# An opening rebuilt: modulation weights from two queues, whole loads of the feature-DFT weights, narrow filler products, the first row pair in halves, weight differences on VectorE

## The chip, the core and the metric

The kernel runs on one core of a Trainium2 chip. It is one launch, and the time is the device time of that launch in microseconds. The kernel before took 716.78 us as the median of three runs (714.04 to 717.35). One further execution was recorded by the hardware profiler; it took 715.7 us from its first to its last instruction, and all views below are of it. Engines are called PE (TensorE's products), PEld (its weight loads), DVE (VectorE), ACT (ScalarE), POOL (GpSimd) and SP (SyncE, which here only issues loads).

## The reference

An adaLN-conditioned block over 2048 rows of 512 features: a Fourier mixing layer, then a SwiGLU layer (1792 hidden columns). The change touches the start of the first.

```
mod = (silu(c) @ w_mod).reshape(c.shape[0], 6, 1, -1)
sa, ca, ga, sb, cb, gb = (mod[:, 0], mod[:, 1], ..., mod[:, 5])
h = layernorm(x) * (1 + ca) + sa
a = einsum("bsd,ed->bse", h, dft_hid_re)        # feature DFT
b = einsum("bsd,ed->bse", h, dft_hid_im)
y = einsum("ts,bse->bte", dft_seq_re, a) - einsum("ts,bse->bte", dft_seq_im, b)   # sequence DFT
x = x + ga * y
h = layernorm(x) * (1 + cb) + sb
x = x + gb * (einsum(silu(h w1) * (h w3), w2))
```

## The kernel before

The work is one long function, `folded`, that writes out the program of all engines; each engine runs its own instructions in the order written, and waits for others by semaphores. It uses symmetries of the DFT: rows are taken in eight *row pairs* k (two sides of 128 rows each, the second the mirror of the first), and the features in four blocks dt of 128. Products in float32 are split into a high part and a low part (a rounded copy, and what is left), so that high x high, high x low and low x high make one product (`PASSES`).

**Loads.** SP issues, in this order: the condition `cc`, the rows x0 of pair 0, four blocks `wmr` of 512 KB of modulation weights (`load_wm`, L212), the feature-DFT weights `w` of block 0 (`load_hid`, L222), x1, w of blocks 1 to 3, x2 and x3. A block w[dt] is 128 partitions x 1024 numbers: 512 of the real matrix `wdr`, 512 of the imaginary `wdi`. In memory `w[i]` lies as 128 rows, each with two parts q of 512 numbers; `load_hid` takes every second row, part 0 to partitions 0 to 63 and part 1 to partitions 64 to 127, by two loads per matrix. For x4 to x7 one side comes from SP and the mirrored side by a gather that GpSimd issues (`load_mirror`, L165; L170).

**The opening's steps.** `mod_scale(v, h)` multiplies modulation weights by silu(c) (one ACT and three DVE instructions per v), `mod_sum(v)` sums over partitions on PE (L303) and writes the shift (v = 0) and the scale (v = 1) to `mod1` (L310). Filler products, `keep_warm` (L270), keep PE occupied meanwhile. For a row pair: statistics (`norm_stats`, L433), root, inverse, scaling, `turn_rows` (transposes on PE, L469), `modulate_rows` (L485 on ACT, L487 on DVE: `hm`), `mirror_sums` (`hs`: sum and difference of the two sides), `sum_highs` and `sum_lows` (`hh`, `hl`), `mirror_part` (`h1`). For a block of w: `w_highs` (ACT, `wu`), `w_lows` (DVE, L90 and L383), `w_minus` (ACT, `wn`), `differ_w` (POOL, L399 and L404, `wd`). `hid_product(k, dt)` (L533) then makes the low columns of the feature DFT: for k's first block a product with zeros clears the bank (L528), and for each half m (sum, difference) three passes follow. `hid_mirror` (L569) makes the high columns, `hid_difference` (L550) the correction with `wd`.

**The order.** The first pair's norm, turning and modulation sums are written out by hand. The rest of the opening is a table of tasks, each with a rank, needs and a cost per engine; `arrange` (L1284) takes again and again the task of lowest rank among those that can begin soonest by these costs and by due times for what is loaded (`at`, `clear`), and writes it. So costs and due times decide the order of the instructions on an engine, not when they run. After the opening, the sequence DFT (L723), the second norm and the SwiGLU layer (L100) follow.

Of the kernel before, what the change touches and what calls it, by code (L numbers as in the profile page):

```python
# [15 lines left out]
P = 128  # L16
# [26 lines left out]
def folded(nc, pools, c, cp, wmr, wmc, x, xt, ctr, cti, wdr, wdi, w1, w3, w2, out):  # L43
# [30 lines left out]
    def flat(t):  # L74
        return t.rearrange("p a b -> p (a b)")
# [10 lines left out]
    def copy(dst, src, scale=1.0):  # L86
        nc.scalar.activation(dst, src, AF.Copy, scale=scale)  # L87
# [122 lines left out]

    wm = {}

    def load_wm(v):
        for k in range(2):
            wm[v, k] = take(F32, "wmr")
            nc.sync.dma_start(wm[v, k], wmr[v, k])


    HD = ((0, 1), (1, 1), (0, 0), (1, 0))
# [2 lines left out]
    def load_hid(dt):  # L222
        i, par = HD[dt]
        raw_w[dt] = take(F32, "w")
        for m, w in enumerate((wdr, wdi)):
            for q in range(2):
                nc.sync.dma_start(raw_w[dt][q * 64 : (q + 1) * 64, m, :], w[i][par::2, q])

    nc.sync.dma_start(cc, cp)
    load_x(0)  # L230
    load_wm(1)
    load_wm(0)
    load_hid(0)
    load_x(1)
    for dt in range(1, ND):
# [30 lines left out]
    nc.vector.memset(onesf, 1.0)  # L266
    warm = bank(7)

    def keep_warm(count):

        for _ in range(count):
            nc.tensor.matmul(warm, onesf[:, :P], onesf, start=True, stop=True)

    sc = consts.tile([P, ND], F32, name="sc")
    nc.scalar.activation(sc, cc, AF.Silu)
# [24 lines left out]
    def mod_sum(v):  # L300

        for dt in range(ND):
            nc.tensor.matmul(  # L303
                mod_acc[:, v * ND + dt : v * ND + dt + 1],
                hid_cols(wm[v, 0][:, 0, :], dt),
                onesf[:, :1],
                start=True,
                stop=True,
            )
        nc.vector.tensor_scalar(  # L310
            mod1[:, v, :], mod_acc[:, v * ND : (v + 1) * ND], float(v), None, op0=OP.add
        )
        for h in range(2):
            give(wm.pop((v, h)))

# [76 lines left out]
    def differ_w(dt):  # L392
        r = quarters(raw_w[dt])
        if dt % 2 == 0:
            wd[dt // 2] = take(F32R, "wd")
        dd = wd[dt // 2][:, dt % 2, :].rearrange("p (a n) -> p a n", a=2)

        def pool(out, a, b, op):
            nc.gpsimd.tensor_tensor(out=out, in0=a, in1=b, op=op)  # L399

        if HD[dt][1]:
            pool(dd[:, 0, :], r[:, 0, 1, :], r[:, 0, 0, :], OP.add)
            pool(r[:, 1, 1, :], r[:, 1, 1, :], r[:, 1, 0, :], OP.add)
            nc.gpsimd.tensor_scalar(dd[:, 1, :], r[:, 1, 1, :], -1.0, None, op0=OP.mult)  # L404
        else:
            pool(dd[:, 0, :], r[:, 0, 1, :], r[:, 0, 0, :], OP.subtract)
            pool(dd[:, 1, :], r[:, 1, 0, :], r[:, 1, 1, :], OP.subtract)
        give(raw_w.pop(dt))

    def check_w(n):  # L410
# [83 lines left out]
            sides(hs[k])[:, :, m, :], sides(hm[k])[:, :, 0, :], sides(hm[k])[:, :, 1, :]  # L494
        )

    def sum_highs(k):
        hh[k] = take(F32R, "hh")
        copy(flat(hh[k]), flat(hs[k]))

    def sum_lows(k):
        hl[k] = take(F32R, "hl")
        minus(flat(hl[k]), flat(hs[k]), flat(hh[k]).bitcast(F32))
        give(hs.pop(k))

    def mirror_part(k):

# [13 lines left out]
    def halves(b):  # L521
        return b.rearrange("p (a n) -> p a n", a=2)

    def hid_product(k, dt):
        if dt == 0:

            hb[k] = bank(4 + k % 2)
            nc.tensor.matmul(  # L528
                hb[k], nought, flat(wt[0])[:, :N], start=True, stop=False, skip_group_check=True
            )  # L530
        for m in range(2):
            for n, (a, b) in enumerate(PASSES):
                nc.tensor.matmul(  # L533
                    halves(hb[k])[:, m, :],
                    sides((hh, hl)[a][k])[:, dt, m, :],
                    wu[dt][:, b, m, :],
                    start=False,
                    stop=dt % 2 == 1 and n == 2,
                    skip_group_check=True,
                )  # L540
# [20 lines left out]
    def hid_mirror(k, high):  # L561

        h1b[k, high] = to = bank(6 + high)
        u = h1[k].rearrange("p a (d n) -> p a d n", d=ND)
# [713 lines left out]
    def task(name, rank, needs, fn, **ways):  # L1278


        pending.append((rank, name, needs, fn, ways))

    def arrange(hand_over=0.1, window=0.3):
        while pending:  # L1284
            ready = []
            for at, (rank, name, needs, fn, ways) in enumerate(pending):
                if any(n not in ends for n in needs):
                    continue
                for engine, us in ways.items():
                    begin = clear.get(engine, 0.0)  # L1290
                    for n in needs:
                        end, by = ends[n]
                        begin = max(begin, end if by == engine else end + hand_over)
                    ready.append((begin, rank, us, at, engine))
            soon = min(r[0] for r in ready) + window
            begin, rank, us, at, engine = min(
                (r for r in ready if r[0] <= soon), key=lambda r: (r[1], r[0] + r[2])
            )
            _, name, _, fn, ways = pending.pop(at)
            ends[name] = (begin + us, engine)  # L1300
            clear[engine] = begin + us
            fn(engine) if len(ways) > 1 else fn()
# [78 lines left out]
    for k in range(NK):  # L1381
# [21 lines left out]
                )  # L1403
        for dt in range(ND):
            task(
                f"mod{k}.{dt}", r + RANK["mod"] + 0.1 * dt, ["mod", *[f"turn{n}" for n in both]],
                lambda e, k=k, dt=dt: modulate_rows(k, dt, e), ACT=0.45, DVE=0.43,
            )
        for m in range(2):
# [5 lines left out]
        task(f"hh{k}", r + RANK["hh"], sums_done, lambda k=k: sum_highs(k), ACT=0.97)  # L1415
        task(f"hl{k}", r + RANK["hl"], [f"hh{k}"], lambda k=k: sum_lows(k), DVE=1.16)
        task(f"h1{k}", r + RANK["h1"], sums_done, lambda k=k: mirror_part(k), ACT=0.55)
        for dt in range(ND):
# [1011 lines left out]
```

## Time and profile before

| | |
|---|---|
| median of 3 runs | 716.78 us |
| profiled execution, span | 715.7 us |
| mean granted clock of PE | 0.978 |
| PE busy | 689.8 us (96%) |
| DVE busy | 551.9 us (77%) |
| ACT busy | 428.7 us (60%) |
| POOL busy | 129.8 us (18%) |
| first product of the feature DFT | 24.07 us from the start |
| first product of the sequence DFT | 93.25 us from the start |

A row of a *timeline* or of the costliest groups reads: start and length in us (or busy time), engine, line, operation, output <- inputs by the program's names, shapes, and in square brackets the idle time before it with the engine or load that ended it. `bank` is an accumulator of PE. A number behind an x counts instructions. A row of *windows* gives for a stretch of the span the busy time of each engine, PE's granted clock as a fraction of full speed, the share of the 16 DMA engines that was busy, and GB/s. The *chain of waits* is followed back from the last instruction to what released it.

### The profile page before, as it was taken

What the parts mean: (1) busy time and instruction counts of PE and PEld (TensorE: products, weight loads), DVE (VectorE), ACT (ScalarE), POOL (GpSimd) and SP (SyncE); (2) the same over time, 40 slices, a digit from 0 to 9 for tenths busy, and PEclk for the clock granted to TensorE, in tenths of its full rate; (3) what the DMA queues carried; (4) which work ended last, traced back from release to release, by engine and by line L of the source; (5) the groups of instructions that cost most, each with busy time, mean ns of one, the idle gap of its engine ahead of it and who ended that gap; (6) DMA issues with size and microseconds to landing.
All of it is one profiled execution on the core that took longest, in us unless ns stands there. A gap on an engine that the chain in (4) does not pass through costs nothing.

```text
span 715.7 us, 8791 instructions
## 1 busy us (share of the span) xinstructions
PE 689.8 (96%) x3094; PEld 563.4 (79%) x3094; DVE 551.9 (77%) x873; ACT 428.7 (60%) x700; POOL 129.8 (18%) x147
## 2 busy tenths in 40 slices
PE   7699999999999999999999999999999999999995
PEld 3587888888888888777888788787788888888784
DVE  4889887999899977679997887897666456664663
ACT  4687975455453665646677767667665655656420
POOL 3520073443435000100100101011010101101000
PEclk8599999999999999999999999999999999999998
DMA  8630089878588530442667566376854748447503
GB/s 245 225 116 3 5 289 355 280 257 294 172 312 266 171 142 31 75 76 86 130 164 161 133 148 137 69 127 136 266 115 91 154 76 182 87 91 129 165 1 122
DMA packets 37956, 108.93 MB, mean 152 GB/s; under 512 B 4880, under 2 KB 5136, under 8 KB 37904
## 3 DMA queue, kind: packets, MB, share of 16 engines
q0 software_dynamic: 12352, 43.00, 28.8%
q1 hardware_dynamic: 25552, 65.29, 27.7%
q8 instruction: 26, 0.43, 0.2%
q14 instruction: 26, 0.21, 0.1%
HBM read 76.81 MB, written 33.55 MB: 154 GB/s over the span
## 4 chain that ended last, share of the span: by engine, by line
PE 60%; issue 23%; DVE 6%; DMA 4%; ACT 4%; POOL 2%; SPq 1%; POOLq 0%; ACTq 0%; DVEq 0%
PE bank L100 32%; PE bank L723 25%; POOL sum L1119 2%; PE bank L533 2%; DMA sum<-y 2%; DMA x<-in_x 1%; PE bank L569 1%; DMA wmr<-in_wmr 1%; DVE hl L90 1%; ACT hm L485 1%; PE bank L469 1%; DVE hs L90 1%; ACT y L317 0%; DVE hm L487 0%; ACT ho L87 0%
## 5 line engine op out<-in xcount | busy, mean ns | idle before, releaser
L100 PE MATMUL bank<-hf,w2h 128*128 128x512 f32 (+1 forms) x452 | 140.8, 391 | 1.0 <-ACT y L317 0.7
L1119 POOL DMA_DIRECT2D sum<-y x48 | 41.1, 856 | 390.9 <-ACT y L317 373.1
L100 PEld LDWEIGHTS bank<-hf,w2h 128*128 128x128 f32 x452 | 84.3, 188 | 22.8 <-DVE hf L90 3.4
L100 PE MATMUL bank<-hf,w2l 128*128 128x512 f32 (+1 forms) x226 | 87.6, 388 | 0.0
L317 ACT ACTIVATE y<-bank,gb 128x512 f32<-128x512 f32 x96 | 65.0, 683 | 19.1 <-PE bank L100 18.4
L87 ACT ACTIVATE hf<-v 128x512 fp32r<-128x512 f32 x56 | 35.3, 630 | 67.2 <-DVE v L96 62.6
L93 DVE TENSOR_TENSOR v<-bank,x 128x512 f32<-128x512 f32 x36 | 24.7, 686 | 34.8 <-PE bank L100 34.8
L170 POOL DMA_INDIRECT re<-in_ctr,mirror x32 | 36.5, 1142 | 73.8 <-PE bank L569 37.6
L723 PE MATMUL bank<-bh,us 128*128 128x512 f32 x128 | 49.9, 390 | 0.0
L723 PE MATMUL bank<-bh,ul 128*128 128x512 f32 x128 | 49.8, 389 | 0.0
L723 PE MATMUL bank<-d,us 128*128 128x512 f32 x128 | 49.8, 389 | 0.0
L723 PE MATMUL bank<-d,uh 128*128 128x512 f32 x128 | 49.8, 389 | 0.0
L723 PE MATMUL bank<-l,us 128*128 128x512 f32 x128 | 49.8, 389 | 0.0
L723 PE MATMUL bank<-l,uh 128*128 128x512 f32 x128 | 49.8, 389 | 0.0
L93 DVE TENSOR_TENSOR x<-bank,x 128x512 f32<-128x512 f32 x36 | 24.8, 688 | 32.4 <-PE bank L100 28.7
L100 PEld LDWEIGHTS bank<-hf,w2l 128*128 128x128 f32 x226 | 42.4, 188 | 8.4
L90 DVE TENSOR_TENSOR hf<-v,hf 128x512 fp32r<-128x512 f32 x56 | 38.5, 687 | 12.2 <-ACT hf L87 12.1
L1197 ACT ACTIVATE v<-v 128x512 f32<-128x512 f32 x36 | 22.8, 632 | 38.9 <-DVE v L93 38.9
L87 ACT ACTIVATE x<-bank 128x512 f32<-128x512 f32 x72 | 41.4, 587 | 7.1 <-PE bank L100 6.5
L170 POOL DMA_INDIRECT im<-in_cti,mirror x32 | 35.1, 1096 | 34.4 <-DVE l L90 9.7
L100 PE MATMUL bank<-h2h,w1h 128*128 128x512 f32 x80 | 31.8, 397 | 1.5 <-ACT h2h L87 1.5
L100 PE MATMUL bank<-h2l,w1h 128*128 128x512 f32 x80 | 32.0, 400 | 0.8 <-DVE h2l L90 0.8
(243 smaller groups left out, 1785.7 us busy)
## 6 DMA issues: line engine op xcount, KB each, us to landing
sum<-y POOLq DMA_DIRECT2D x48, 512.0 KB, 5.4
w<-in_w SPq DMA_DIRECT2D x42, 512.0 KB, 4.5
re<-in_ctr SPq DMA_DIRECT2D x32, 256.0 KB, 5.5
im<-in_cti SPq DMA_DIRECT2D x32, 256.0 KB, 4.9
wmc<-in_wmc SPq DMA_DIRECT2D x8, 512.0 KB, 6.9
xr<-in_xt SPq DMA_DIRECT2D x8, 512.0 KB, 7.6
sum<-xr SPq DMA_DIRECT2D x8, 512.0 KB, 6.6
x<-in_x SPq DMA_DIRECT2D x12, 256.0 KB, 4.5
```

Source lines behind the costliest of these rows:

```text
L87: nc.scalar.activation(dst, src, AF.Copy, scale=scale)
L90: nc.vector.tensor_tensor(out=dst, in0=a, in1=b, op=OP.subtract)
L93: nc.vector.tensor_tensor(out=dst, in0=a, in1=b, op=OP.add)
L100: nc.tensor.matmul(acc, lhs[a], rhs[b], start=first and n == 0, stop=last and n == len(PASSES) - 1, skip_group_check=more,)
L170: nc.gpsimd.indirect_dma_start(dst, None, rows, bass.IndirectOffsetOnAxis(ap=at, axis=0))
L317: nc.scalar.activation(dst, src, AF.Identity, scale=by)
L469: nc.tensor.transpose(turned[k][dt // 2][:, at : at + P], hid_cols(xz[k][:, side, :], dt), anti if side and where(k)[1] else ident,)
L485: nc.scalar.activation(dst, src, AF.Identity, bias=sa, scale=ca1)
L533: nc.tensor.matmul(halves(hb[k])[:, m, :], sides((hh, hl)[a][k])[:, dt, m, :], wu[dt][:, b, m, :], start=False, stop=dt % 2 == 1 and n == ...
L723: nc.tensor.matmul(acc[what, e], lhs, rhs, start=begin and i == 0, stop=(end or (turn and what == "x")) and i == len(terms) - 1, skip_grou ...
L1119: nc.gpsimd.dma_start(sums[t, d // 2], y, accum_op=OP.add)
L1197: behind(k != 0 or q == 0, lambda: nc.scalar.activation(v, src, AF.Silu))
```

## The change

1. The blocks `wmr` of v = 1 are loaded from ACT's queue, as the program's first instructions; those of v = 0 from SP's, the second in two pieces.
2. `load_hid` loads each matrix's part of a block with one load of 128 rows. Its source is the same memory with the two parts q as the outer dimension.
3. The modulation sums are reordered: v = 1 is scaled and summed first, then the clearing of pair 0's bank (with zeros instead of w), a filler, then v = 0, whose result is written in four instructions of a column each. GpSimd's `differ_w` becomes eight DVE instructions, and its rank moves behind pair 1's sums.
4. For row pair 0, highs, lows and products are made for each half m apart, and the low pass is a task of its own.
5. Until the first `hid_mirror`, the planner puts narrow fillers (128 columns instead of 512) ahead of a PE task when PE would be idle by its costs. Due times change.

```diff
-    def load_wm(v):
+    def load_wm(v, queue, apart):
         for k in range(2):
             wm[v, k] = take(F32, "wmr")
-            nc.sync.dma_start(wm[v, k], wmr[v, k])
+            if k and apart:
+                for n in range(2):
+                    queue.dma_start(wm[v, k][:, n, :], wmr[v, k, :, n, :])
+            else:
+                queue.dma_start(wm[v, k], wmr[v, k])
...
         for m, w in enumerate((wdr, wdi)):
-            for q in range(2):
-                nc.sync.dma_start(raw_w[dt][q * 64 : (q + 1) * 64, m, :], w[i][par::2, q])
-
+            nc.sync.dma_start(raw_w[dt][:, m, :], w[i][par::2].rearrange("p q n -> q p n"))
+
+    load_wm(1, nc.scalar, False)
     nc.sync.dma_start(cc, cp)
     load_x(0)
-    load_wm(1)
-    load_wm(0)
+    load_wm(0, nc.sync, True)
...
-    def keep_warm(count):
+    def keep_warm(count, width=N):
         for _ in range(count):
-            nc.tensor.matmul(warm, onesf[:, :P], onesf, start=True, stop=True)
+            nc.tensor.matmul(
+                warm[:, :width], onesf[:, :P], onesf[:, :width], start=True, stop=True
+            )
...
         if HD[dt][1]:
-            pool(dd[:, 0, :], r[:, 0, 1, :], r[:, 0, 0, :], OP.add)
-            pool(r[:, 1, 1, :], r[:, 1, 1, :], r[:, 1, 0, :], OP.add)
-            nc.gpsimd.tensor_scalar(dd[:, 1, :], r[:, 1, 1, :], -1.0, None, op0=OP.mult)
+            plus(dd[:, 0, :], r[:, 0, 1, :], r[:, 0, 0, :])
+            nc.vector.scalar_tensor_tensor(
+                dd[:, 1, :], r[:, 1, 1, :], -1.0, r[:, 1, 0, :], op0=OP.mult, op1=OP.subtract
+            )
         else:
-            pool(dd[:, 0, :], r[:, 0, 1, :], r[:, 0, 0, :], OP.subtract)
-            pool(dd[:, 1, :], r[:, 1, 0, :], r[:, 1, 1, :], OP.subtract)
+            minus(dd[:, 0, :], r[:, 0, 1, :], r[:, 0, 0, :])
+            minus(dd[:, 1, :], r[:, 1, 0, :], r[:, 1, 1, :])
...
+            if engine == "PE" and filling:
+                keep_warm(max(0, int((begin - clear["PE"] - 0.1) / 0.23)), P)
...
+    keep_warm(1)
     nc.gpsimd.memset(flat(zero), 0.0)
     copy(nought, zero[:, 0, :P])
-    for v in (1, 0):
-        for h in range(2):
-            mod_scale(v, h)
+    for h in range(2):
+        mod_scale(1, h)
+    mod_sum(1)
     clear_z()
-    for v in (1, 0):
-        mod_sum(v)
-        keep_warm(2 if v else 1)
-    give(first_tmp)
+    hid_begin(0)
+    keep_warm(1)
+    for h in range(2):
+        mod_scale(0, h)
+    mod_sum(0)
...
-    at(13.6, "mod")
-    at(12.0, "turn0.0", "turn0.1")
-    at(14.0, "x1")
+    at(10.0, "turn0.0", "turn0.1")
     for dt in range(ND):
-        at((12.1, 16.0, 18.0, 20.0)[dt], f"w{dt}")
-    for k in range(2, 4):
-        at(22.0 + 2.0 * (k - 2), f"x{k}")
-    for engine in clear:
-        clear[engine] = 13.6
+        at(13.3 + 0.25 * dt, f"modc{dt}")
+        at((13.2, 15.9, 17.2, 18.6)[dt], f"w{dt}")
+    for k in range(1, 4):
+        at((14.5, 20.0, 21.3)[k - 1], f"x{k}")
+    clear.update(PE=13.6, DVE=13.9, ACT=11.0, POOL=9.0, SP=9.0)
...
-        task(f"wd{dt}", -6 + 2 * dt, [f"wl{dt}"], lambda dt=dt: differ_w(dt), POOL=3.0)
+        task(f"wd{dt}", 1 + 0.5 * dt, [f"wl{dt}"], lambda dt=dt: differ_w(dt), DVE=0.9)
...
+        if k == 0:
+            for m in range(2):
+                task(f"hh0.{m}", r + RANK["hh"], [f"sum0.{m}"], lambda m=m: sum_highs(0, m), ACT=0.63)
+                task(f"hl0.{m}", r + RANK["hl"], [f"hh0.{m}"], lambda m=m: sum_lows(0, m), DVE=0.69)
```

How this moves instructions, on three engines. SP, from x0 to x2, before (`in_wdr` and `in_wdi` are the two feature-DFT matrices in memory, `in_wmr` the modulation weights):

```order
L205 DMA x_86<-in_x 128x1x512
L207 DMA x_86<-in_x 128x1x512
L216 DMA wmr_89<-in_wmr 128x1024
...
L227 DMA w_97<-in_wdr 64x512 x2
L227 DMA w_97<-in_wdi 64x512 x2
L205 DMA x_102<-in_x 128x1x512
L207 DMA x_102<-in_x 128x1x512
L227 DMA w_105<-in_wdr 64x512 x2
...
L227 DMA w_115<-in_wdi 64x512 x2
L205 DMA x_120<-in_x 128x1x512
```

and of the change:

```order
L205 DMA x_90<-in_x 128x1x512
L207 DMA x_90<-in_x 128x1x512
L220 DMA wmr_93<-in_wmr 128x1024
L218 DMA wmr_95<-in_wmr 128x512 x2
L230 DMA w_98<-in_wdr 128x1x512
L230 DMA w_98<-in_wdi 128x1x512
L205 DMA x_101<-in_x 128x1x512
L207 DMA x_101<-in_x 128x1x512
L230 DMA w_104<-in_wdr 128x1x512
...
L230 DMA w_110<-in_wdi 128x1x512
L205 DMA x_113<-in_x 128x1x512
```

Two of the four modulation loads are gone from SP, and each pair of 64-row loads of w is one of 128 rows; the order of what is left is the same. DVE, from the statistics of pair 2's first side (x_120 before, x_113 in the change) to pair 1's lows, before:

```order
L433 BN_STATS st_0_278<-x_120 128x6
L434 BN_AGGR mv_276<-st_0_278 128x2
L433 BN_STATS st_1_291<-x_120 128x6
L434 BN_AGGR mv_276<-st_1_291 128x2
L90 TENSOR_TENSOR wu_273<-w_115,wu_273 128x256
L383 SCALAR_TENSOR_TENSOR wu_273<-w_115,wu_273 128x256
...
L93 TENSOR_TENSOR hs_320<-hm_287 128x4x128
L90 TENSOR_TENSOR hs_320<-hm_287 128x4x128
...
L90 TENSOR_TENSOR hl_358<-hs_320,hh_335 128x1024
```

and of the change:

```order
L441 BN_STATS st_0_299<-x_113 128x6
L442 BN_AGGR mv_297<-st_0_299 128x2
L441 BN_STATS st_1_305<-x_113 128x6
L442 BN_AGGR mv_297<-st_1_305 128x2
L90 TENSOR_TENSOR wu_267<-w_110,wu_267 128x256
L393 SCALAR_TENSOR_TENSOR wu_267<-w_110,wu_267 128x256
...
L90 TENSOR_TENSOR hs_332<-hm_308 128x4x128
L93 TENSOR_TENSOR wd_340<-w_98 128x256
L410 SCALAR_TENSOR_TENSOR wd_340<-w_98 128x256
L93 TENSOR_TENSOR wd_340<-w_104 128x256
L410 SCALAR_TENSOR_TENSOR wd_340<-w_104 128x256
L90 TENSOR_TENSOR hl_357<-hs_332,hh_348 128x1024
```

In both, the last block's lows (w_115, w_110) stand behind pair 2's statistics; four of the eight differences now stand between pair 1's sums and its lows, and four behind. PE of the change, from the first modulation sum to pair 0's second block (`tmp` is the filler's operand, `bank_20` the bank of pair 0):

```order
L308 MATMUL bank_15_142<-tmp_131,wmr_85 128x1 x4
L541 MATMUL bank_20_186<-z_144,nought 128x512
L275 MATMUL bank_14_133<-tmp_131 128x512
L308 MATMUL bank_15_142<-tmp_131,wmr_93 128x1 x4
L275 MATMUL bank_14_133<-tmp_131 128x128 x16
L551 MATMUL bank_20_186<-wu_201,hh_221 128x256 x2
L275 MATMUL bank_14_133<-tmp_131 128x128
L551 MATMUL bank_20_186<-wu_201,hl_223 128x256
L551 MATMUL bank_20_186<-wu_201,hh_221 128x256 x2
L275 MATMUL bank_14_133<-tmp_131 128x128
L551 MATMUL bank_20_186<-wu_201,hl_223 128x256
L275 MATMUL bank_14_133<-tmp_131 128x128 x6
```

Before, one wide filler and the clearing product stood between the second modulation sum and the first product; now sixteen narrow fillers do.

More of the change, by code (lines that the diff above doesn't have):

```diff
@@ L309, in mod_sum @@
             )
-        nc.vector.tensor_scalar(
-            mod1[:, v, :], mod_acc[:, v * ND : (v + 1) * ND], float(v), None, op0=OP.add
-        )
+        for at in (slice(0, ND),) if v else [slice(dt, dt + 1) for dt in range(ND)]:
+            nc.vector.tensor_scalar(
+                mod1[:, v, at],
+                mod_acc[:, v * ND : (v + 1) * ND][:, at],
+                float(v),
+                None,
+                op0=OP.add,
+            )
         for h in range(2):
@@ L396, in differ_w @@
         dd = wd[dt // 2][:, dt % 2, :].rearrange("p (a n) -> p a n", a=2)
-        def pool(out, a, b, op):
-            nc.gpsimd.tensor_tensor(out=out, in0=a, in1=b, op=op)
         if HD[dt][1]:
-            pool(dd[:, 0, :], r[:, 0, 1, :], r[:, 0, 0, :], OP.add)
-            pool(r[:, 1, 1, :], r[:, 1, 1, :], r[:, 1, 0, :], OP.add)
-            nc.gpsimd.tensor_scalar(dd[:, 1, :], r[:, 1, 1, :], -1.0, None, op0=OP.mult)
-        else:
-            pool(dd[:, 0, :], r[:, 0, 1, :], r[:, 0, 0, :], OP.subtract)
-            pool(dd[:, 1, :], r[:, 1, 0, :], r[:, 1, 1, :], OP.subtract)
+            plus(dd[:, 0, :], r[:, 0, 1, :], r[:, 0, 0, :])
+            nc.vector.scalar_tensor_tensor(
+                dd[:, 1, :], r[:, 1, 1, :], -1.0, r[:, 1, 0, :], op0=OP.mult, op1=OP.subtract
+            )
+        else:
+            minus(dd[:, 0, :], r[:, 0, 1, :], r[:, 0, 0, :])
+            minus(dd[:, 1, :], r[:, 1, 0, :], r[:, 1, 1, :])
         give(raw_w.pop(dt))
@@ L495, in mirror_sums, with part_of, sum_highs, sum_lows @@
         )
[L497 to L504, printed above, removed]
+    def part_of(t, m):
+        return flat(t) if m is None else sides(t)[:, :, m, :]
+    def sum_highs(k, m=None):
+        if not m:
+            hh[k] = take(F32R, "hh")
+        copy(part_of(hh[k], m), part_of(hs[k], m))
+    def sum_lows(k, m=None):
+        if not m:
+            hl[k] = take(F32R, "hl")
+        minus(part_of(hl[k], m), part_of(hs[k], m), part_of(hh[k], m).bitcast(F32))
+        if m != 0:
+            give(hs.pop(k))
     def mirror_part(k):
@@ L522, in halves, with hid_begin, hid_product @@
         return b.rearrange("p (a n) -> p a n", a=2)
[L524 to L532, printed above, removed]
+    def hid_begin(k):
+        hb[k] = bank(4 + k % 2)
+        nc.tensor.matmul(
+            hb[k], nought, flat(wt[0] if k else zz)[:, :N], start=True, stop=False, skip_group_check=True
+        )
+    def hid_product(k, dt, ms=range(2), ns=range(3)):
+        if dt == 0 and k:
+            hid_begin(k)
+        for m in ms:
+            for n in ns:
+                a, b = PASSES[n]
                 nc.tensor.matmul(
@@ L563, in hid_mirror @@
         h1b[k, high] = to = bank(6 + high)
+        if filling:
+            filling.clear()
+            give(first_tmp)
         u = h1[k].rearrange("p a (d n) -> p a d n", d=ND)
@@ L1281, in task @@
         pending.append((rank, name, needs, fn, ways))
+    filling = [True]
     def arrange(hand_over=0.1, window=0.3):
@@ L1405, in folded @@
             task(
-                f"mod{k}.{dt}", r + RANK["mod"] + 0.1 * dt, ["mod", *[f"turn{n}" for n in both]],
+                f"mod{k}.{dt}", r + RANK["mod"] + 0.1 * dt, [f"modc{dt}", *[f"turn{n}" for n in both]],
                 lambda e, k=k, dt=dt: modulate_rows(k, dt, e), ACT=0.45, DVE=0.43,
@@ L1414, in folded @@
         sums_done = [f"sum{n}" for n in both]
-        task(f"hh{k}", r + RANK["hh"], sums_done, lambda k=k: sum_highs(k), ACT=0.97)
-        task(f"hl{k}", r + RANK["hl"], [f"hh{k}"], lambda k=k: sum_lows(k), DVE=1.16)
         task(f"h1{k}", r + RANK["h1"], sums_done, lambda k=k: mirror_part(k), ACT=0.55)
-        for dt in range(ND):
+        if k == 0:
+            for m in range(2):
+                task(f"hh0.{m}", r + RANK["hh"], [f"sum0.{m}"], lambda m=m: sum_highs(0, m), ACT=0.63)
+                task(f"hl0.{m}", r + RANK["hl"], [f"hh0.{m}"], lambda m=m: sum_lows(0, m), DVE=0.69)
+            for dt in range(ND):
+                after = ["odd0"] if dt > 1 else []
+                for m in range(2):
+                    task(
+                        f"prodh0.{dt}.{m}", r + RANK["prod"] + 2 * dt + m / 2, [f"hh0.{m}", f"wl{dt}", *after],
+                        lambda dt=dt, m=m: hid_product(0, dt, (m,), (0, 1)), PE=0.24,
+                    )
+                    task(
+                        f"prodl0.{dt}.{m}", r + RANK["prod"] + 2 * dt + m / 2,
+                        [f"hl0.{m}", f"prodh0.{dt}.{m}"],
+                        lambda dt=dt, m=m: hid_product(0, dt, (m,), (2,)), PE=0.12,
+                    )
+                task(f"prod0.{dt}", -99, [f"prodl0.{d}.{m}" for d in range(dt + 1) for m in range(2)], lambda: None, NONE=0.0)
+        else:
+            task(f"hh{k}", r + RANK["hh"], sums_done, lambda k=k: sum_highs(k), ACT=0.97)
+            task(f"hl{k}", r + RANK["hl"], [f"hh{k}"], lambda k=k: sum_lows(k), DVE=1.16)
+        for dt in range(ND if k else 0):
             needs = [f"hl{k}", f"wl{dt}"]
```

## The prediction

> **What bounds the kernel now.** I read the stretches first, because the change touches only the opening. The columns are the stretch in us, then its length, the busy us and instructions of PE, PEld, DVE, ACT and POOL, the granted clock of PE, the share of the 16 DMA engines and GB/s.
>
> ```profile
> 0.00:6.00 6.00, 3.39 (x4) 1.51 (x5) 1.94 (x7) 2.77 (x3) 2.98 (x16) 1.00 0.46 113
> 6.00:12.00 6.00, 3.52 (x13) 1.60 (x11) 4.24 (x9) 3.18 (x6) 0.00 (x0) 1.00 1.02 371
> 12.00:18.00 6.00, 6.00 (x19) 3.93 (x19) 2.00 (x4) 1.25 (x3) 2.84 (x3) 0.51 1.03 250
> 18.00:24.00 6.00, 2.91 (x6) 1.24 (x6) 5.29 (x10) 3.42 (x8) 5.74 (x7) 0.50 0.73 228
> 24.00:30.00 6.00, 4.26 (x18) 3.97 (x19) 5.86 (x15) 4.09 (x9) 4.92 (x5) 0.50 0.98 321
> 30.00:36.00 6.00, 5.31 (x23) 4.83 (x23) 4.12 (x11) 5.22 (x9) 0.07 (x1) 0.50 0.36 118
> 200.00:300.00 100.00, 100.00 (x443) 82.75 (x442) 88.68 (x142) 54.44 (x90) 14.65 (x16) 1.00 0.50 162
> ```
>
> From about 36 us on PE is the bound and stays full; its order there is the same in both kernels. Up to 30 us the loads fill the DMA engines (shares 0.98 to 1.03, one gap) and PE waits. So whatever the opening gains or loses arrives at the end nearly whole. The chain of waits says through what the opening runs (start, length, work):
>
> ```profile
> 3.18 6.25 DMA wmr<-in_wmr
> 9.45 7.84 DMA x<-in_x
> ...
> 19.09 2.62 DMA w<-in_wdi
> 21.72 1.21 DVE hs L90
> ...
> 25.35 1.15 DVE hl L90
> 26.54 1.22 PE bank L533 x4
> ...
> 91.54 1.71 PE bank L533 x12
> 93.25 1.84 PE bank L723 x8
> ```
>
> Modulation weights, the feature-DFT weights w (last issued at 19.09, in at about 21.7), row pair 0's sums and its lows, the first products, and at 93.25 the sequence stage starts. The w loads are on this path, with a few us to spare: the last block's first use on VectorE came at 29.55, behind the statistics of x2.
>
> ```profile
> 27.92 0.69 DVE L433 BATCH_NORM_STATS2 st<-x 128x6 f32<-128x512 f32 x1
> 28.64 0.18 DVE L434 BATCH_NORM_AGGREGATE mv<-st 128x2 f32<-128x6 f32 x1
> 29.55 0.43 DVE L90 TENSOR_TENSOR wu<-w,wu 128x256 fp32r<-128x256 f32 x1
> 29.89 0.42 DVE L383 SCALAR_TENSOR_TENSOR wu<-w,wu 128x256 fp32r<-128x256 f32 x1
> ```
>
> **The w loads.** The change replaces sixteen loads of 64 rows by eight of 128. The bytes stay, 2 MB in rows of 2 KB, and SP issues eight times less. What differs is the source's shape. Before, its outermost dimension was 64 (rows); the rearranged source has 2 halves outermost, then 64 rows, then 512 numbers. The x loads also put 128 rows into place, but their source has the 64 outermost and the 2 inside.
>
> ```profile
> x<-in_x SPq DMA_DIRECT2D x12, 256.0 KB, 4.5
> wmr<-in_wmr SPq DMA_DIRECT2D x4, 512.0 KB, 6.7
> w<-in_wdr SPq DMA_DIRECT2D x8, 128.0 KB, 4.6
> w<-in_wdi SPq DMA_DIRECT2D x8, 128.0 KB, 4.2
> q1 hardware_dynamic: 4304, 8.39, 46.5%
> ```
>
> Every load of the opening (these rows: count, KB each, median us to landing; the last: packets and MB of the first 60 us) moves whole rows, 8.39 MB in 4304 packets, about 2 KB each. It is dealt out to the DMA engines row by row, and in all of them 16 divides the outermost dimension of both sides, 64 or 128. So no row shows what a load with 2 outermost does. There are two bounds. If the dealing ignores the source's shape, each engine gets 8 rows of a 128-row load, as in the x loads. If it goes along the outermost dimension, there are two parts, and two engines carry 64 rows each while fourteen stand still. The nearest row, x, has as many rows as the new loads and lands in 4.5 us, but it has 64 outermost and so fits both readings. Cutting a load into equal parts is simplest along its outermost dimension, and every load shown could be cut so; I take two engines, and keep sixteen as a rival.
>
> [...]
>
> What a row costs on an engine is bounded by two stretches.
>
> ```profile
> 28.50:30.50 2.00, 2.00 (x11) 1.95 (x9) 1.74 (x6) 0.56 (x1) 1.27 (x2) 0.50 1.05 418
> 14.00:18.00 4.00, 4.00 (x11) 2.15 (x9) 0.82 (x2) 0.83 (x2) 2.84 (x3) 0.50 1.01 256
> ```
>
> With all sixteen full (share 1.05), x rows and gathers move at 418 GB/s, or 26 GB/s an engine: 2 KB in 0.08 us. From 14 to 18, with the 64-row w loads, it is 256 GB/s, 16 an engine, 0.13 us. I take 0.08, since with two engines at work nothing else crowds the memory.
>
> Now the sum. What comes ahead of w is cc, x0 and four modulation blocks of 512 KB, 2.6 MB: 0.68 MB by 6 us (113 GB/s) and the other 1.9 at 371 GB/s make about 11 us, two queues or one. From there both engines of the pair carry 8 loads x 64 rows = 512 rows x 0.08 = 41 us. Between them come x1, 16 rows an engine, 1.3 us, and GpSimd's four gathers x4 to x7, 32 rows an engine, 2.6 us; these now start early, since what stood ahead of them on GpSimd goes away.
>
> ```profile
> L399 POOL TENSOR_TENSOR wd<-w 128x256 fp32r<-128x256 f32 x6 | 5.8, 989 | 11.2 <-DMA w<-in_wdr 11.2
> 24.56 1.25 POOL L170 DMA_INDIRECT x<-in_x,mirror  x1 [0.17 <-issue]
> ```
>
> So the last w block lands at 11 + 41 + 1.3 + 2.6, about 56 us, where before it was 21.7. x2 stands behind it in SP's queue and lands 16 rows later, at 57.2. VectorE's order has both statistics of x2 ahead of the last lows (unchanged), so: second side's statistics 57.5 to 58.4 (0.69 + 0.18), the two lows to about 59.1. Before they ended at 29.89 + 0.42 = 30.3. The shift is 28.8 us. Everything behind keeps its order, so nothing there makes up for it: at 30 us before, as at 59 after, row pair 0's third block of products has just run and the fourth waits for w.
>
> **The differences move from GpSimd to VectorE.** Ten instructions (6 + 2 of L399, 2 of L404) become eight of 128x256 on VectorE, placed between row pair 1's sums and its lows. Rows of the same shape:
>
> ```profile
> 24.59 0.43 DVE L90 TENSOR_TENSOR wu<-w,wu 128x256 fp32r<-128x256 f32 x1
> 24.94 0.41 DVE L383 SCALAR_TENSOR_TENSOR wu<-w,wu 128x256 fp32r<-128x256 f32 x1
> 25.27 1.21 DVE L90 TENSOR_TENSOR hl<-hs,hh 128x1024 fp32r<-128x1024 f32 x1
> ```
>
> From start to start that is 0.35 and 0.33 us, so 8 x 0.34 = 2.7 us. Bounds: 0, if VectorE has the slack there (4.12 of 6 us busy from 30 to 36), and 2.7, because lows and high parts of pair 1 queue behind them. I take 2.7: four of the eight stand directly ahead of pair 1's lows, and the rest ahead of what pair 2 needs.
>
> **The rest of the change** is worth something only if w is early. Modulation of the first row pair starts once the second sum is done:
>
> ```profile
> 11.82 1.62 PE L303 MATMUL bank<-tmp,wmr 128*128 128x1 f32 x8 [2.11 <-DVE wmr L296]
> 13.30 3.76 PE L272 MATMUL bank<-tmp 128*128 128x512 f32 x4
> 18.60 0.16 DVE L310 TENSOR_SCALAR mod<-bank 128x4 f32<-128x4 f32 x1 [3.77 <-PE bank L303]
> 19.49 1.42 PE L528 MATMUL bank<-wu,nought 128*128 128x512 f32 x1
> 20.95 0.85 DVE L93 TENSOR_TENSOR hs<-hm 128x512 f32<-128x512 f32 x1
> 24.07 0.80 PE L533 MATMUL bank<-wu,hh 128*128 128x256 f32 x2 [3.16 <-ACT hh L87]
> ```
>
> A wide filler is two instructions here (four for two fillers), 1.88 us. Ahead of the second sum now stand one of them and the nought product, 1.88 + 1.42 = 3.3 us, where two stood, 3.76: half a us, and the first sum starts earlier by what the second queue brings, up to another us. Of the two sums of one shape the one beside GpSimd's work took 1.21 against 0.85, 0.4 back. Halves let the first product wait for half a highs and half a lows instruction, 0.6 of the 1.21. Together that is 2 to 3 us of the first product's 24.07. But the first product also waits for w's first block: 11 us + 128 rows x 0.08 and some gathers make 21 to 24, and the second block comes 10 us later. So this gain is covered by the wait for w and counts nothing. The narrow fillers stand in that same wait, and cost nothing either.
>
> **Sum.** 28.8 + 2.7 = 31.5 us on the profiled 715.7 us is 747.2. The median shown is 1.1 above the profiled execution: 748.
>
> **Rivals.** *The pair at the slower pace.* Rows on two engines cost 0.13 us, as from 14 to 18 us: 512 x 0.13 = 67 instead of 41, 26 more, about 774. For it: those were these very w loads. Against it: POOL, PE and many queues were at work together then, and the rate rose to 418 with the same row size later.
>
> *All sixteen engines.* The loads are spread as x is, w lands by 22 as before or a us earlier (SP's eight issues less), and the opening's gain is real: the first product near 21.5 instead of 24.07, 2 to 3 us, with the 0.50 clock of 12 to 36 us partly lifted by the fillers, 2 more, less up to 2.7 on VectorE: 1.5 to 4.5 faster, about 714. It decides if a w load's time to landing stays under 6 us. The DMA share stays near 1 between 12 and 24 in this case. This is the case on the other side.
>
> *Sixteen engines, but the fillers stand in front.* The planner put 16 narrow fillers ahead of the first product, reckoned at 0.23 us each, 3.7. At the granted 0.50 one takes a quarter of a wide one's 1.88, 0.47, and sixteen 7.5: 3.8 us late, more than the 2 to 3 gained. With part of VectorE's 2.7 the time is 716 to 719. For it: the 0.50 rows from 12 to 36. Against it: PE waits 3.16 us in front of the first product now, room for most of the excess.
>
> **How the numbers follow.** Two engines at 0.08 to 0.1 us a row 0.74, two engines at the slow pace 0.12, sixteen with a gain 0.07, sixteen without 0.07. The predicted time is the likeliest case's, 748. Down, its own bounds are 2.7 (VectorE's slack), 2.6 (gathers that go ahead while the modulation weights still load) and 1.3 (x1 the same), 741; 2 to 3 us of row pair 0's gain may survive, 738, and I go to 736. Up, 0.1 us a row gives 10 more, 758; up to half-way into the slow pace, 770. 0.5% of 716.8 is 3.6 us, about what a measurement of this kernel can tell from no change. Faster by more: only the gain case at its upper end, 0.05. Within: the rest of it and the filler case, 0.09. Slower: both two-engine cases, 0.86.
>
> **What would show it.** In the profile after, w loads of 128 KB that need 6 us or more from issue to landing where 4.2 to 4.6 stood, and the later ones tens of us. Between 24 and 54 us a DMA share of 0.12 to 0.15 and some 50 GB/s (2 x 26) where 0.98 and 321 stood. ACT's copies of the second to fourth w block each released by a DMA, about 10 us apart; PE idle most of 25 to 56 at a clock of 0.50. The last lows at about 59, the sequence stage's first product (93.25 before) at about 125, and from there to the end the same length as before, within 1 us. GpSimd's gathers from 4 us on, and no GpSimd work at L399. The prediction is wrong if w's last block lands before 30 us; then the time is one of the sixteen-engine cases. It is wrong in size if it lands well before 50 or after 62.

## The result, and the profile after

The changed kernel takes 749.43 us as the median of four runs (749.16 to 750.08); the kernel before, run beside it, 716.82 us. The ratio is 1.0469, with a 95% interval from 1.044 to 1.0498: slower by 33 us. The profiled execution has a span of 747.4 us where 715.7 stood. (The device time of a profiled execution is about 1.8 us above its span, in every run below, so the spans compare directly.)

The windows of the changed kernel, with the same columns as before:

```profile
12.00:18.00 6.00, 5.64 (x15) 2.88 (x13) 3.54 (x6) 0.44 (x1) 0.00 (x0) 0.50 0.44 143
18.00:24.00 6.00, 6.00 (x29) 6.00 (x29) 1.14 (x6) 0.65 (x2) 0.00 (x0) 0.50 0.13 50
24.00:30.00 6.00, 4.52 (x35) 4.06 (x33) 4.58 (x9) 3.54 (x7) 0.00 (x0) 0.97 0.14 53
30.00:36.00 6.00, 1.02 (x5) 0.51 (x4) 0.47 (x2) 0.91 (x3) 0.00 (x0) 0.89 0.13 51
...
48.00:54.00 6.00, 0.70 (x4) 0.30 (x2) 0.19 (x1) 0.42 (x1) 0.00 (x0) 0.50 0.71 201
60.00:66.00 6.00, 5.46 (x32) 4.92 (x31) 4.25 (x10) 4.33 (x9) 0.00 (x0) 0.84 0.06 23
```

From 18 to 36 us the DMA engines are busy to 0.13, which is 2 of 16 (0.125), and move 50 GB/s, which is two times 25. PE, VectorE and ACT have little to do from 30 to 60 (PE is busy 4.4 of these 30 us). The chain of waits goes through this stretch on one queue:

```profile
11.57 4.16 SPq L207
...
16.45 5.20 SPq L230
...
31.96 5.09 SPq L230
...
37.10 20.49 DMA w<-in_wdi
57.61 0.02 ACT wu L87
```

L230 is the new load. ACT's copies of the blocks, one for each load, show when the loads land (timeline, ACT):

```profile
18.55 0.42 ACT L87 ACTIVATE wu<-w 128x256 fp32r<-128x256 f32 x1 [6.11 <-DMA w<-in_wdr]
23.77 0.42 ACT L87 ACTIVATE wu<-w 128x256 fp32r<-128x256 f32 x1 [4.80 <-DMA w<-in_wdi]
30.29 0.42 ACT L87 ACTIVATE wu<-w 128x256 fp32r<-128x256 f32 x1 [2.76 <-DMA w<-in_wdr]
35.51 0.42 ACT L87 ACTIVATE wu<-w 128x256 fp32r<-128x256 f32 x1 [4.80 <-DMA w<-in_wdi]
...
57.61 0.42 ACT L87 ACTIVATE wu<-w 128x256 fp32r<-128x256 f32 x1 [5.38 <-DMA w<-in_wdi]
```

The two loads of a block land 5.22 us apart, 64 rows of 0.0815 us. The last is in at 57.6, and VectorE finishes its lows behind the statistics of x2 at 60.21 + 0.42 = 60.6, against 30.3 before:

```profile
58.27 0.69 DVE L441 BATCH_NORM_STATS2 st<-x 128x6 f32<-128x512 f32 x1 [10.08 <-DMA x<-in_x]
...
60.21 0.42 DVE L393 SCALAR_TENSOR_TENSOR wu<-w,wu 128x256 fp32r<-128x256 f32 x1
```

The sequence stage's first product, before and then in the changed kernel (timeline, PE):

```profile
93.08 0.40 PE L723 MATMUL bank<-bh,us 128*128 128x512 f32 x1
```

```profile
125.71 0.39 PE L744 MATMUL bank<-bh,us 128*128 128x512 f32 x1
```

It starts 32.6 us later; from there to the end it is 621.7 us against 622.6. So the whole loss lies ahead of the sequence stage: 30.3 us up to the last lows, 2.3 behind them.

### The profile page after: what moved, and what is told of

Read it like the earlier page. It is cut to its first block, busy times and chain, and to the rows that moved or that the text cites. A ratio compares the mean times of both kernels' runs of the same rounds, so it can differ in the third digit from the quotient of the medians.

```text
span 747.4 us, 8886 instructions
## 1 busy us (share of the span) xinstructions
PE 698.3 (93%) x3150; PEld 571.6 (76%) x3150; DVE 550.7 (74%) x879; ACT 432.9 (58%) x707; POOL 118.5 (16%) x137
## 3 DMA queue, kind: packets, MB, share of 16 engines
q1 hardware_dynamic: 25168, 64.24, 25.6%
q10 hardware_dynamic: 288, 1.05, 0.4%
## 4 chain that ended last, share of the span: by engine, by line
PE 75%; DVE 8%; ACT 7%; SPq 4%; DMA 3%; issue 2%; ACTq 0%; DVEq 0%
PE bank L100 48%; PE bank L744 24%; SPq L230 3%; DMA w<-in_wdi 3%; PE bank L551 1%; ACT xc L888 1%; PE bank L590 1%; DMA x<-in_x 1%; DVE ul L90 1%; SPq L205 1%; DVE xc L96 1%; ACT y L327 1%; DVE v L96 1%; SPq L207 1%; ACT hh L87 1%
## 5 line engine op out<-in xcount | busy, mean ns | idle before, releaser
L170 POOL DMA_INDIRECT im<-in_cti,mirror x32 | 33.6, 1049 | 35.8 <-PE bank L744 10.4
```

The costliest lines, as they stand in the source:

```text
L170: nc.gpsimd.indirect_dma_start(dst, None, rows, bass.IndirectOffsetOnAxis(ap=at, axis=0))
```

## The experiments

All but the third and fifth start from the changed kernel. Times are medians; ratios are to the kernel before on the same chip, with 95% intervals.

| run | what differs | us | ratio |
|---|---|---|---|
| e1 | w by sixteen loads of 64 rows | 716.57 | 1.0025 (1.0008 to 1.0042) |
| e2 | w by eight loads of 128 rows, 128 outermost | 717.10 | 1.0023 (1.0008 to 1.0039) |
| e3 | kernel before, only with the new loads | 743.02 | 1.0374 (1.0344 to 1.0404) |
| e4 | w by eight loads, 4 outermost | 730.18 | 1.0201 (1.0174 to 1.0228) |
| e5 | kernel before, only with e2's loads | 713.25 | 0.9975 (0.9960 to 0.9989) |
| e6 | e2 without narrow fillers | 718.02 | 1.0031 (1.0017 to 1.0045) |
| e7 | e2, all modulation weights from SP behind x0 | 715.16 | 1.0004 (0.9992 to 1.0016) |
| e8 | e2, differences on GpSimd | 715.22 | 0.9989 (0.9974 to 1.0003) |
| e9 | e7 and e8 together | 713.01 | 0.9959 (0.9942 to 0.9975) |
| e10 | e9 with fewer fillers | 712.32 | 0.9943 (0.9925 to 0.9961) |
| e11 | e1's sixteen loads out of e2's layout | 719.08 | 1.0043 (1.0023 to 1.0063) |

### The loads: e1 to e4

e1 puts the old loads back into the changed kernel:

```diff
-            nc.sync.dma_start(raw_w[dt][:, m, :], w[i][par::2].rearrange("p q n -> q p n"))
+            for q in range(2):
+                nc.sync.dma_start(raw_w[dt][q * 64 : (q + 1) * 64, m, :], w[i][par::2, q])
```

> The changed kernel with w loaded as before, by sixteen loads of 64 rows (outermost dimension 64). Theory (a load whose source has 2 outermost is carried by two engines, and that alone is the loss): w is in by about 22 us, the first product stands at 21 to 23 us, the time is 713 to 717. Rival (the loss is elsewhere in the change: gathers that start early, modulation weights from ACT's queue, differences on VectorE): 740 or more.

716.57 us: some 32 us of loss (by the ratios) are gone with these two lines. The rest of the change loses a little, 0.25%. The first product stands at 23.93, later than the 21 to 23 expected.

e2 keeps eight loads of 128 rows. The matrices are given once more to the kernel, laid out by the host so that a load's 128 rows follow each other:

```diff
-            nc.sync.dma_start(raw_w[dt][:, m, :], w[i][par::2].rearrange("p q n -> q p n"))
+            nc.sync.dma_start(raw_w[dt][:, m, :], w[i, par])       # w: whr, whi, [2, 2, 128, 512]
```

> The changed kernel with the same eight loads of 128 rows, but w laid out in memory so that the 128 rows of a load are its outermost dimension. Theory (it is the 2 outermost, not the size of the load or its number): within 1 us of the kernel with sixteen loads, 713 to 717, w loads land in 4 to 6 us. Rival (a load of 128 rows of w lands late whatever its form): 745 to 750.

717.10 us. The same number of loads, the same rows, bytes and places in the chip's memory as in the changed kernel, and the loss is gone; so it is not the size of the load. Only the places in the source memory and the outermost dimension differ. One expectation failed: from issue to landing the w loads needed 7.6 and 8.3 us (medians of the two matrices), not 4 to 6, so that time alone doesn't tell the two cases apart. The windows of e2 have all DMA engines at work up to 24 us (shares 1.05 and 1.02):

```profile
12.00:18.00 6.00, 5.84 (x15) 2.91 (x14) 3.60 (x6) 1.33 (x3) 0.00 (x0) 0.50 1.05 385
18.00:24.00 6.00, 6.00 (x34) 6.00 (x35) 4.06 (x12) 3.48 (x7) 0.00 (x0) 0.59 1.02 381
24.00:30.00 6.00, 5.98 (x52) 5.79 (x51) 5.82 (x17) 5.19 (x12) 0.00 (x0) 1.00 0.15 53
```

e3 changes only the loads in the kernel before (the reverse of e1's diff).

> The kernel before with only the eight new w loads. Theory: the last block lands at 13 + 41 + 1.3, about 55 us, the last lows end near 58.5 where 30.3 stood, 745 (743 to 748), that is some 3 to 4 less than the changed kernel, which has the differences on VectorE and the early gathers besides. Rival (the new loads hurt only together with the rest of the change): 716 to 720.

743.02 us, at the lower edge of what was expected. The new loads alone make a loss of 27.5 us, without the early gathers, ACT's queue or VectorE's differences. That is 5.1 less than the changed kernel's 32.6, not 3 to 4. Its copies on ACT again come 5.2 us apart:

```profile
28.43 0.42 ACT L87 ACTIVATE wu<-w 128x256 fp32r<-128x256 f32 x1 [3.85 <-DMA w<-in_wdr]
33.64 0.42 ACT L87 ACTIVATE wu<-w 128x256 fp32r<-128x256 f32 x1 [4.79 <-DMA w<-in_wdi]
38.85 0.42 ACT L87 ACTIVATE wu<-w 128x256 fp32r<-128x256 f32 x1 [3.33 <-DMA w<-in_wdr]
```

Its last lows, and its sequence stage's first product (timeline, VectorE and PE):

```profile
58.23 0.42 DVE L382 SCALAR_TENSOR_TENSOR wu<-w,wu 128x256 fp32r<-128x256 f32 x1
```

```profile
118.65 0.40 PE L722 MATMUL bank<-bh,us 128*128 128x512 f32 x1
```

The last lows end at 58.65, 28.3 us later than in the kernel before, as expected (58.5). But the sequence stage starts only 25.6 us later: behind the last lows e3 makes up 2.8 us, where the changed kernel loses 2.3 more. These are distances in one trace each.

e4 is e2 with each load's rows laid out so that the source's outermost dimension is 4 (32 rows inside):

```diff
+            nc.sync.dma_start(raw_w[dt][:, m, :], w[i, par].rearrange("p g n -> g p n"))   # w: [2, 2, 32, 4, 512]
```

> The changed kernel with w laid out so that the source of each 128-row load has 4 outermost, then 32 rows. Theory (as many engines as the outermost dimension): a load lands every 2.6 us instead of 5.2, 20.5 us for the eight, last block at about 35, last lows near 39, about 727 (724 to 730). Rival (any source that isn't in the order of its rows goes through two engines, or through one path of fixed speed): 749. Rival (4 outermost is already spread over all sixteen): 713 to 717.

730.18 us. ACT's copies of the second block, and the window from 18 to 24 us:

```profile
23.38 0.42 ACT L87 ACTIVATE wu<-w 128x256 fp32r<-128x256 f32 x1
25.99 0.42 ACT L87 ACTIVATE wu<-w 128x256 fp32r<-128x256 f32 x1 [2.19 <-DMA w<-in_whi]
```

```profile
18.00:24.00 6.00, 6.00 (x32) 6.00 (x33) 4.86 (x14) 4.19 (x8) 0.00 (x0) 0.55 0.26 99
```

The two loads of a block land 2.61 us apart, half of 5.22. The share is 0.26 (4 of 16 is 0.25) at 99 GB/s, four times 25. So 2 outermost kept 2 engines busy (0.13 in the changed kernel) and 4 kept 4, at one price per row (5.22 / 64 and 2.61 / 32, both 0.0816 us). That rules the first rival out: this source is out of the order of its rows too, and it isn't bound to two engines. The time lies just above the theory's range (724 to 730): the copies of the last two blocks begin at 28.99, 32.23, 36.28 and 38.77, up to 4 us apart and not 2.6; why was not tried.

### Why the rest gains nothing: e6 to e8

In e2 the first product stands at 24.67 us (24.07 before), though GpSimd's work no longer lies beside VectorE's. Its chain of waits, up to that product:

```profile
1.91 5.70 DMA x<-in_x
...
19.59 5.33 PE bank L275 x32
24.91 0.24 PE bank L551 x2
```

Two things stand there: x0, whose second side lands at 7.6 us (before, its statistics began at 6.10), and the sixteen narrow fillers (two instructions each, 5.33 us).

e7 takes ACT's queue away:

```diff
-    load_wm(1, nc.scalar, False)
     nc.sync.dma_start(cc, cp)
     load_x(0)
+    load_wm(1, nc.sync, False)
     load_wm(0, nc.sync, True)
```

> The changed kernel with the loads of 128 rows, 128 outermost, and all modulation weights from SP's queue behind x0, v = 1 first. Theory (the loads on ACT's queue take half the DMA engines from x0, so it lands 1.5 us late and drags norm and sums along): x0's second side in by 6.2 instead of 7.6, modulation done near 18 instead of 19.6; the first product still behind the fillers, 23 to 23.5; 715 to 716. Rival (the second queue brings the modulation weights earlier): 718 or more.

The statistics of x0's second side, and the end of modulation, in e2 and then in e7 (timeline, VectorE):

```profile
7.64 0.69 DVE L441 BATCH_NORM_STATS2 st<-x 128x6 f32<-128x512 f32 x1 [0.17 <-DMA x<-in_x]
...
19.62 0.35 DVE L316 TENSOR_SCALAR mod<-bank 128x1 f32<-128x1 f32 x4 [1.96 <-PE bank L308]
```

```profile
6.13 0.69 DVE L441 BATCH_NORM_STATS2 st<-x 128x6 f32<-128x512 f32 x1 [0.38 <-DMA x<-in_x]
...
17.34 0.36 DVE L316 TENSOR_SCALAR mod<-bank 128x1 f32<-128x1 f32 x4 [1.96 <-PE bank L308]
```

x0 lands 1.5 us earlier and modulation ends 2.3 us earlier; the first product stands at 22.51. The time is 715.16, some 1.4 us lower by the ratios; the two intervals overlap, so the gain in time is likely and not certain, while the trace shows the place. The second queue's megabyte moves beside x0, and all steps up to modulation wait for x0 first. How much of the engines it takes from x0 can't be read from these rows, and a second queue that starts behind x0 was not tried.

e6 leaves out the narrow fillers (the call in the planner is dropped).

> The changed kernel with the loads of 128 rows, 128 outermost, and without narrow fillers. Theory A (the sixteen fillers stand 1.3 us in front of the first product and the clock comes anyway): first product at 23.4 instead of 24.7, about 716. Theory B (they bring the full clock at 24 us, and without them it comes at 33 or later): the products of pair 0 take twice as long, the sequence stage starts 1 to 2 us later than 93.3, 718 to 719.

Theory B. The first product comes earlier, at 23.46, but the clock from 24 to 30 us is 0.50 instead of 1.00, and the sequence stage starts at 95.30 instead of 93.16. The medians differ by less (718.02 and 717.10, intervals overlap), so the fillers bring 0 to 2 us. By the traces the full clock is worth more than the 1.2 us that sixteen of them stand in front of the first product; the times don't show it.

e8 gives the differences back to GpSimd: `differ_w` and its task as before.

> The changed kernel with the loads of 128 rows, 128 outermost, and the weight differences on GpSimd again, ahead of its gathers. Theory (the eight instructions on VectorE cost 2.3 to 2.7 us, as between the last lows and the sequence stage in the changed kernel): pair 1's lows follow its sums at once, 714.5 to 715. Rival (VectorE has slack there, and GpSimd's work slows VectorE's beside it): 717 or more.

715.22 us, 0.34% or 2.4 us less than e2 by the ratios, and just above what was expected. The place is another than the theory names. Row pair 1's second sum and its lows, in e2's timeline of VectorE and then in e8's:

```profile
32.51 0.68 DVE L90 TENSOR_TENSOR hs<-hm 128x512 f32<-128x512 f32 x1
33.11 0.42 DVE L93 TENSOR_TENSOR wd<-w 128x256 fp32r<-128x256 f32 x1
...
34.12 0.41 DVE L410 SCALAR_TENSOR_TENSOR wd<-w 128x256 fp32r<-128x256 f32 x1
34.45 1.22 DVE L90 TENSOR_TENSOR hl<-hs,hh 128x1024 fp32r<-128x1024 f32 x1
```

```profile
33.66 0.69 DVE L90 TENSOR_TENSOR hs<-hm 128x512 f32<-128x512 f32 x1
...
34.66 1.00 DVE L464 TENSOR_SCALAR x<-x,rs 128x512 f32<-128x512 f32 x2
35.58 1.22 DVE L90 TENSOR_TENSOR hl<-hs,hh 128x1024 fp32r<-128x1024 f32 x1
```

In e2 four differences stand between sum and lows, and four more behind the lows. In e8 the lows do not follow at once either, 1.92 us from start to start against 1.94: the planner now puts row pair 2's inverse and scaling there. So pair 1's lows gain nothing; pair 2 gains. Its transposes on PE start at 35.26 instead of 38.48 and its row sums at 39.47 instead of 41.32, though e8's first product comes later (25.82, 24.67 in e2). In e2 PE waits for pair 2 at `hid_mirror`:

```profile
44.28 1.20 PE L590 MATMUL bank<-wu,h 128*128 128x512 f32 x4 [2.05 <-ACT h L87]
```

Between 15 and 95 us PE waits 3.1 us for ACT's copies `h` in e2 and 0.3 in e8. Whether the eight instructions themselves or the order that the planner makes around them costs the time was not tried apart. The rival's second half is seen too, without setting the time: two scaling instructions on VectorE (L301) take 2.23 us beside GpSimd's work in e8 (POOL is busy 5.82 of 6 us from 12 to 18) and 1.54 in e2 (POOL 0.00).

### What beats both kernels: e5, e9, e10

> The kernel before with only the eight loads of 128 rows from the layout with 128 outermost. Theory (the loads of before were not what its opening waited for; the modulation sums were): w is in some 3 us earlier, the first product stays at 24 us, the time within 1 us of before. Rival (the faster loads are worth their gain): 3 us less, 712 to 713.

713.25 us, between the theory and its rival. The new loads alone, with the matrices laid out for them by the host, make the kernel before faster by 0.25%. That the rate gains it (below) is likely; the first product stands at 23.48, the last lows end at 28.61 instead of 30.31.

> The changed kernel with the loads of 128 rows (128 outermost), all modulation weights from SP's queue behind x0, and the differences on GpSimd. Theory (the two losses lie at different places, x0's landing and VectorE between pair 1's sums and lows, so both come back): about 2 us below each of the two alone, 713 to 713.5, sequence stage's first product near 89.5. Rival (both are one slack on the same path): 715, as either alone.

> The same with the planner's narrow filler reckoned at 0.34 us (5.33 us for sixteen, measured) instead of 0.23: ten instead of sixteen ahead of the first product. Theory (six fillers of 0.33 us stand in front of it): first product up to 1.3 us earlier than with sixteen, time 0 to 1 us lower, 712 to 713. Rival (fewer fillers lose the full clock): 0.5 to 1.5 us higher.

e9, at 713.01, has both losses back, as the theory said; e10, with this one edit more, 712.32:

```diff
-                keep_warm(max(0, int((begin - clear["PE"] - 0.1) / 0.23)), P)
+                keep_warm(max(0, int((begin - clear["PE"] - 0.1) / 0.34)), P)
```

Its first product is at 22.40 (24.43 in e9), 2.0 us earlier where at most 1.3 were expected, and its sequence stage starts at 89.01 (90.22). Its 0.9943 is the best of all; from e9 it can't be told by the intervals.

### The rate: e11

```diff
+            for q in range(2):
+                nc.sync.dma_start(raw_w[dt][q * 64 : (q + 1) * 64, m, :], w[i, par, q * 64 : (q + 1) * 64])
```

> The changed kernel with sixteen loads of 64 rows, as before, but out of the layout in which a load's rows follow each other in memory. It tells why the loads of 128 rows came at 385 GB/s between 12 and 18 us and those of 64 rows, every second row in memory, at 280. If the number of rows (64 partitions) sets it: 250 to 280 GB/s again. If the distance of the rows in memory sets it: 370 to 390 GB/s. The time is 715 to 717.5 either way.

From 13 to 17 us, in e11, e1 and e2, one row each:

```profile
13.00:17.00 4.00, 3.30 (x13) 1.60 (x11) 2.55 (x5) 0.78 (x2) 0.00 (x0) 0.85 1.06 287
```

```profile
13.00:17.00 4.00, 2.74 (x11) 1.43 (x11) 2.73 (x5) 0.83 (x2) 0.00 (x0) 0.78 1.06 291
```

```profile
13.00:17.00 4.00, 4.00 (x12) 2.54 (x11) 1.97 (x5) 0.83 (x2) 0.00 (x0) 0.50 1.05 384
```

The engines are full in all three (1.05, 1.06), but sixteen loads of 64 rows move 287 to 291 GB/s and eight of 128 rows 384. Where the rows lie in memory made no difference to the rate here (287 in e11, 291 in e1). Whether it is the 64 rows, the 64 partitions or the number of loads was not tried. The time, 719.08, lies 1.6 us above what was expected; why it is not 716.57 as in e1 is open (the two intervals overlap).

## Why the prediction was right

**The number.** 749.43 us against 748, and 747.4 against 747.2 in the span. What is left, about 1 us, is the step from span to median: 2.0 us here, 1.1 in the kernel before.

**What bounds.** PE is nearly full from the sequence stage on (before, 206.9 of 206.9 us from 93.1 to 300 and 395 of the 400 after), and what the opening loses arrives nearly whole: 32.6 us at its end, 31.7 in the span. It does not stay full from 36 us on, as the prediction has it from the row of 200 to 300 us: from 54 to 66 us it is busy 5.21 and 5.23 of 6 us before, and up to the sequence stage the chain of waits changes between PE, VectorE and ACT. So there is room between 36 and 93 us in which a delay can be made up, or grow.

**The w loads, two engines.** Right, and shown: a DMA share of 0.13 and 50 GB/s, 0.0815 us a row against the 0.08 taken. The prediction took this reading against a nearest row that fitted both, and e4 is the proof that was missing: in the four cases tried, the number of busy engines followed the outermost dimension, 2 (share 0.13), 4 (0.26, e4) or, at 64 and 128, all sixteen (1.05 in e1 and in e2). That all eight loads go through the same two engines, as the sum takes it, no run shows: a share says how many are busy, not which. Shown is that the loads land one after another, the two of a block 5.22 us apart, at a share of 0.13. One load of 128 rows in place of two halves isn't enough by itself: with 128 outermost it gains 0.25% (e5, 0.9975), with 2 outermost it costs 3.74% (e3, 1.0374).

**The terms.** The w loads begin at about 13.3 us (18.55 - 5.22) where the prediction has 11 and, for the gathers, 2.6; x1 takes the 1.3 counted (30.29 - 23.77 - 5.22). The last load landed at 57.6 against 56, mainly because the last block's two loads took 5.87 and 5.80 us instead of 5.22, while x2 to x7 were moving too (share 0.71 from 48 to 54 us); how they disturb the pair is open. The shift up to the last lows is 30.3 against 28.8. Behind it the shift grows by 2.3, where 2.7 stood for VectorE's differences. But this agreement is partly luck, for 2.3 is a balance. The prediction says that nothing behind the last lows makes up for the delay; e3 makes up 2.8 there. So the rest of the change costs about 5.1 there, of which the differences are 2.4 by e8, over the whole kernel. A possible part of the 2.8 is the clock: before, it is at 0.50 up to 36 us, 5.7 past the last lows, and at 1.00 from there; in e3 it is at 0.50 up to 60, 1.4 past them, and no window here shows where it rises after that. Whether this makes the difference was not tried, and what makes up the remainder of the 5.1 is open. The program from the sequence stage on gave 0.9 back. So 31.5 were forecast on the span and 31.7 measured, with misses of 1.5 and 1.3 us that nearly cancel.

**The cover.** That row pair 0's work hides in the wait for w was right in sum. But its own numbers were off: the first product stood at 27.06, not 21 to 24, since the second half of block 0, at 23.8, stands ahead of the row sums on VectorE, with the statistics of x1 behind it. And the clock was at 0.97 from 24 to 30 us and 0.89 to 36, and only from then to 60 at the forecast 0.50. In e3, which has no narrow fillers, it was 0.50 from 18 to 60.

**The rivals.** The case of sixteen engines with a gain (714) would have been wrong. Of the 2 us that it counts for a clock lifted by the fillers, which no row of before shows, e2 and e6 show the lift (1.00 and 0.50 from 24 to 30 us) and 2.1 us at the start of the sequence stage, but only 0.9 in the medians. e1 and e2 land in the case without a gain (716 to 719). Its reason was only partly the one given. The fillers stand 1.2 us in the way (24.67 against 23.46 in e6), not 3.8. Sixteen took 5.33 us, not 7.5: the clock rises at about 23 us, while they run (0.59 over 18 to 24 us in e2, 1.00 from there), and mostly at a clock of 0.50 one costs 0.41 to 0.43, not 0.47 (sixteen took 6.56 in e9, ten 4.29 in e10). The rest lies where the prediction had a gain or less: the modulation weights of the second queue, "up to another us" earlier, go with an x0 that is late and cost about 1.4 us (e7), and the differences cost 2.4 (e8), where that case had part of 2.7. By the traces they do so through row pair 2: pair 1's lows, which the prediction names first, start no sooner without them.

## What to carry to other kernels

Before two loads are merged into one, look at the outermost dimension of the source as the load is written: with 2 there, 14 of 16 DMA engines had nothing of these loads to do, and the profile shows it as a busy share of 0.13, 2 of 16. Lay the data out so that a load's rows are its outermost dimension; the same merge then gained 0.25% (e5). And what starts loading on a second queue can move beside what the first step waits for: look in the trace whether that now lands later (here 7.6 instead of 6.1 us).

## What was not expected of the hardware

The loads that two engines carry held up the queue that issues them. The two issues of x1 on SP take 0.57 and 0.56 us before; in the changed kernel the loads behind the first w block look like this (timeline, SP):

```profile
6.62 4.90 SPq L205 DMA_DIRECT2D x<-in_x  x1
11.57 4.16 SPq L207 DMA_DIRECT2D x<-in_x  x1
15.77 0.64 SPq L230 DMA_DIRECT2D w<-in_wdr  x1
16.45 5.20 SPq L230 DMA_DIRECT2D w<-in_wdi  x1
21.70 5.09 SPq L230 DMA_DIRECT2D w<-in_wdr  x1
```

From the second load of block 1 on, an issue of w lasts nearly as long as a load on the pair takes, 5.1 to 5.2 us against 5.22, and x1, whose source has 64 outermost, is held in the same way, 4.90 and 4.16 us. What exactly SP waits for there was not tried.
